# A new list of steps, chunks turned by DMA and a second way out of PSUM in a fused H3 + FFN kernel

## The chip, the cores and the metric

The kernel runs on one core of one Trainium2 chip. The metric is the device time of one execution in microseconds (us). A profiled execution gives the span from the first to the last instruction and, beside it, its own device time, which also holds the little that lies around the span.

## The reference

Sequence length S = 2048, width D = 640, hidden width F = 1728, everything in bf16 at the borders. The input x is normalised once (xn) and used twice: as the gate of a long convolution and as the input of a feed-forward network (FFN).

```python
xn = layernorm(A_q)                                   # [2048, 640]
# A: short convolution of k with 4 taps, times v, then a long convolution over the sequence, times xn
k_shift = sum_t shift(A_k, t) * A_shift_k[:, t]
kv = k_shift * A_v
y  = irfft(rfft(kv padded to 4096) * rfft(A_ssm_k padded to 4096))[:2048].astype(bf16)
s  = xn * (y + kv * A_ssm_D)
# B: FFN
g  = silu(gelu_tanh(xn @ B_w1 + B_b1) @ B_w2 + B_b2)
out = A_q + s * g
```

## The kernel before, in words

The sequence is laid out as 128 partitions by 16 rows (`x_v = ... "(p j) d -> p j d"`), so "row n" is a [128, 640] tile. Four consecutive rows make a chunk, c = 0 to 3, and the FFN works chunk by chunk. One large SBUF tile `mem` of 111 rows of 640 bf16 holds nearly everything. PSUM is the tile `ps` of 8 banks.

The long convolution is done as a discrete Fourier transform split into two stages by matrix products, since 4096 points are 16 x 256:

- **F1 of the filter** (K side). `cl` loads the filter in five pieces, `d` adds A_ssm_D to its first column, `kt{n}` transposes it on TensorE, `kc{n}` copies it out of PSUM, `kf{n}_{h}` multiplies it by the table `ws2` or `ws0` (cosines and sines, built on chip), `ke{n}_{h}` evacuates, `ks{n}` stores to the DRAM scratch scrK. There are 16 n and 2 h.
- **F1 of kv** (U side). `cm{i}_{j}` multiplies k rows by tap j, `ca` adds, `cv` multiplies by v; `uf`, `ue`, `us` are then as on the K side, into scrU.
- **F2, product, inverse 1.** `fl{k}` loads scrK in another order, `ff{g}` and `fe{g}` are the second stage (g from 0 to 31), `mk{k}` copies the result with odd and even partitions swapped (two DMAs from SBUF to SBUF), `ml{k}` loads scrU, `mu{g}` is its second stage, `mp{g}` the complex product on VectorE, `mc{g}` the first inverse stage, `me{g}` its evacuation, `ms{k}` the store to scrC.
- **Inverse 2 and output.** `yl{n}` loads scrC, `y{n}` is four matmuls with the transposed tables G, `yt{n}` (`gate`) multiplies the result by the row of x, `yo` adds the residual row, which `q{c}` loaded again, and `os` stores the row.

The FFN: `st`, `rs`, `nm` are the layernorm of a row. `tt{c}_{k}` transposes chunk c on TensorE (chunk 0: `tx{r}`, row by row), `te` evacuates it. `h{c}_{ft}` is the first FFN product (14 of them for a chunk, five matmuls of 128x512 each; in chunk 0 six are cut into halves `ha`, `hb`), `he` the GELU, `g{c}_{i}` the second product (8 for a chunk, 14 matmuls of 128x320 each), `ge` the SiLU, `gm` the product with the row of x. `it{i}` transposes eight columns' blocks of a table, `ie` evacuates them.

All steps stand in one string, PLAN, in the order in which they are issued. A word such as `ke0_0/17~a` is a step, the row of `mem` where its result goes (/17), the PSUM banks (@0.1), and the engine of an evacuation (~a ScalarE, ~d VectorE). Under `tc.manual_schedule()` each engine runs its own instructions in exactly this order, and waits for data, rows and banks by semaphores. So a step that waits holds up everything behind it on its engine. The loads, the swaps `mk` and the output stores are issued by SyncE (SP) in list order; the scratch stores ks, us and ms by GpSimd (POOL) in list order.

Three lines matter most for what follows. L189 is the evacuation on ScalarE, L190 the one on VectorE (`evac`, whatever the step); L195 holds the matmuls of kf, uf, ff and mu (`mm2`).

Of the kernel before, what the change touches and what calls it, by code (L numbers as in the profile page):

```python
# [41 lines left out]
ge0_3/1 kt3@3 kf5_0@0.1 kc3/16~a g0_5@2 ca0_3 ks2 ke5_0/9~a ke5_1~d cv0 ks5 kf3_0@4.5 ge0_5/0 kf3_1@0.1 cm1_3/7
uf0_0@6.7 ke3_0/70~a g0_4@3 ke3_1~d gm0_5 ks3 cm1_1/17 ue0_0/66~a uf0_1@4.5 cm3_0/21 ge0_4/2 uf1_0@0.1 uf1_1@6.7
ue0_1~a kt6@2 gm0_4 ca1_1 g0_6@3 us0 ue1_0/19~a kc6/72~d ca1_2 ue1_1~a st2_1 kf4_1@4.5 us1 ge0_6/0 kf6_0@0.1 kt7@2
ke4_1~a tt1_2@3 ca1_3 kf6_1@6.7 kc7/6~a ks4 g0_7@4 st2_3 ke6_0/62~a ke6_1~a cv1 te1_2~a ks6 kf7_0@0.1 ge0_7/2 st2_2
kf7_1@6.7 uf2_0@2.3 ke7_0/9~a kt8@5 h1_9@4 ke7_1~a ue2_0/4~d kc8/15~a ks7 st2_0 uf3_1@0.1 he1_9 uf2_1@6.7 kf8_0@2.3
h1_3@5 ue2_1~d rs2 ke8_0/16~d uf3_0@6.7 he1_3 kt9@4 cm2_3/71 h1_4@2 ue3_0/66~a us2 nm2_2 ue3_1~a nm2_0 kt14@3 nm2_3
he1_4 kf8_1@6.7 us3 nm2_1 h1_0@5 kc9/18~a ke8_1~d kc14/70~a kf9_0@0.1 cm2_1/19 ks8 kf9_1@6.7 he1_0 kt10@2 gm0_6
h1_1@4 ca2_1 ke9_0/68~a ke9_1~a gm0_3 kf14_0@0.1 cm3_1/89 h1_12@3 he1_1 ks9 cm4_0/62 kc10/6~a h1_2@5 ke14_0/7~a
ca3_1 he1_12 cm2_2/9 kf10_1@6.7 kf10_0@0.1 he1_2 kt11@4 cm3_2/11 h1_5@2 ke10_0/4~a ca2_2 ke10_1~a h1_6@3 ca3_2  # L50
kc11/23~a ks10 he1_5 ca2_3 kf11_1@0.1 kf11_0@6.7 he1_6 cm3_3/66 h1_10@2 ke11_0/19~a cv2 ke11_1~a kf14_1@4.5 h1_7@3
ca3_3 he1_10 ks11 ke14_1~a cm4_1/15 uf4_0@6.7 uf5_0@0.1 he1_7 ks14 cv3 uf4_1@4.5 kt12@2 ue5_0/17~a h1_8@3 ca4_1
kc12/89~a ue4_0/9~d uf7_0@0.1 ue4_1~a h1_13@2 ue7_0/11~d he1_8 us4 cm4_3/23 kf12_0@6.7 he1_13 uf6_1@4.5 kf12_1@0.1
cv5 ke12_0/71~a kt13@3 h1_11@2 ke12_1~a cm4_2/25 kc13/90~a ks12 gm0_7 uf7_1@6.7 st3_0 uf6_0@0.1 he1_11 g1_0@3
ue6_0/81~a ca4_2 ue6_1~a cm6_3/69 ue7_1~a us6 kf13_0@0.1 uf5_1@4.5 ca4_3 ge1_0/0 us7 uf10_0@6.7 g1_1@2 cm6_0/83 cv4
ue5_1~a st3_3 ke13_0/15~a kt15@3 us5 uf8_0@4.5 ge1_1/1 uf8_1@0.1 st3_2 ue8_0/67~a g1_2@2 ue10_0/4~a gm1_1 kc15/89~a
ue8_1~d cm6_1/101 kf15_1@4.5 us8 ge1_2/2 kf15_0@6.7 uf10_1@0.1 gm1_2 ke15_0/99~a g1_6@3 ca6_1 ke15_1~a st3_1
ue10_1~a ks15 cm6_2/71 uf9_0@6.7 us10 ge1_6/1 uf9_1@4.5 kf13_1@0.1 ue9_0/97~a rs3 gm1_0 tt2_0@2 ca6_2 ue9_1~a g1_5@3
te2_0/6~d ke13_1~a ca6_3 us9 ks13 nm3_1 uf11_1@6.7 ge1_5/2 nm3_0 uf11_0@4.5 g1_4@2 nm3_2 ue11_0/81~a cv6 ue11_1~a
cm7_1/95 us11 uf13_1@0.1 nm3_3 ge1_4/0 uf12_0@4.5 fl5/10 cm7_0/101 uf12_1@6.7 fl0/12 ue12_0/46~a tt2_2@3 fl1/48  # L60
g1_3@2 gm1_4 te2_2~d ue12_1~a fl13/50 ca7_1 fl15/52 us12 fl2/54 cm7_3/56 uf13_0@4.5 ge1_3/0 gm1_5 g1_7@3 cm7_2/89
ue13_0/58~a ue13_1~a gm1_3 ca7_2 us13 ff10@6.7 gm1_6 ge1_7/2 ff0@4.5 ca7_3 ff11@0.1 fe10/4~a tt2_1@2 fe0/99~d fl4/60
fe11~a it0@3 ff2@6.7 te2_1~a cv7 mk5/14 ff1@0.1 ff3@4.5 ie0/62~d fe1~a h2_5@2 fl3/97 fe2/66~d fl8/68 fe3~a mk0/70
gm1_7 uf15_0@0.1 he2_5 uf14_0@6.7 ue15_0/42~d uf14_1@4.5 h2_13@3 mk1/95 ue14_0/81~d uf15_1@0.1 ue14_1~d he2_13
ff4@6.7 h2_6@2 fe4/83~a ue15_1~d us14 ff5@4.5 us15 he2_6 ff9@6.7 fe5~d fl14/44 ff30@0.1 h2_12@3 fe30/85~d mk2/89
ff6@4.5 he2_12 ff8@0.1 h2_11@2 fe8/10~d fl12/46 fe6/12~a fe9~a ff17@4.5 ff31@0.1 he2_11 mk4/48 ff16@6.7 fe31~d
h2_8@3 fe16/87~a fe17~d fl10/16 ff27@0.1 fl6/18 he2_8 ff26@6.7 ml1/20 h2_9@2 fe26/22~d ml0/24 fe27~a ml2/101
ff28@4.5 he2_9 ff29@6.7 fe28/26~d ff7@0.1 ml4/28 fe29~a h2_0@3 fe7~d fl11/30 ff25@4.5 he2_0 ff24@6.7 h2_1@2
fe24/32~d mk3/34 fe25~a h2_7@3 he2_1 ml3/36 ff20@0.1 he2_7 q3/58 ff13@6.7 fe20/81~d ff12@4.5 h2_4@2 fe12/68~a fl7/56
fe13~d mu3@0.1 he2_4 ff21@4.5 mk6/42 mp3/54 mu0@6.7 fe21~a h2_10@3 q1/50 mu5@4.5 mp0/44 he2_10 mu4@0.1 mk10/97  # L70
h2_3@2 mp4/46 fl9/18 mc0@6.7 he2_3 h2_2@3 ml7/16 me0/101~d mc4@0.1 he2_2 ml8/44 mp5/6 mu6@6.7 me4/8~a g2_1@2 mp6/46
mk8/83 mc5@0.1 ge2_1/0 ff14@4.5 me5~d ff15@6.7 g2_2@3 fe14/89~d ms2 fe15~a gm2_1 mc6@0.1 ge2_2/1 ff22@4.5 gm2_2
me6/6~a mu2@6.7 it1@2 mp2/56 ml5/46 fe22/20~a mu1@0.1 q0/77 g2_0@3 ie1~a ml6/24 mp1/8 mk7/66 ff18@4.5 ge2_0/2
mc2@6.7 fe18/95~d mk12/70 mc1@0.1 me2/99~a gm2_0 it3@2 me1~a ff19@4.5 ie3~d q2/72 mc3@6.7 fe19~a ms0 mu8@0.1 me3~d
g2_4@3 mp8/56 ms1 mu7@4.5 ge2_4/0 mu10@6.7 mp7/8 ml15/18 ff23@0.1 g2_3@2 fe23~a mp10/54 mk11/36 mu12@0.1 ge2_3/1
mc7@4.5 mp12/30 mc10@2.3 me7~a tt3_0@6 me10/101~a ms3 mc8@4.5 gm2_3 gm2_4 mc12@0.1 te3_0/54~d me8/34~a mu16@2.3
# [567 lines left out]
```

## Time and profile before

| | before |
|---|---|
| median of 3 runs | 228.1 us (227.66 to 228.65) |
| profiled execution: its own time | 228.88 us |
| profiled execution: span | 227.1 us |
| mean granted TensorE clock | 0.974 |
| TensorE busy | 206.3 us, 91% of the span |
| VectorE busy | 183.6 us, 81% |
| ScalarE busy | 144.0 us, 63% |
| GpSimd busy | 39.1 us, 17% |
| moved by DMA | 57.62 MB, 254 GB/s over the span |

Busy shares are means over the span. A share of the span says little by itself; the stages of the list have different limits, so the table of busy time by stretches and the chain of waits are read beside it. A row of the chain of waits has start, duration and what ran or was waited for; a row of the timeline also has the idle time before it and its releaser.

### The profile page before, as it was taken

What the parts mean: (1) busy time and instruction counts of PE and PEld (TensorE: products, weight loads), DVE (VectorE), ACT (ScalarE), POOL (GpSimd) and SP (SyncE); (2) the same over time, 40 slices, a digit from 0 to 9 for tenths busy, and PEclk for the clock granted to TensorE, in tenths of its full rate; (3) what the DMA queues carried; (4) which work ended last, traced back from release to release, by engine and by line L of the source; (5) the groups of instructions that cost most, each with busy time, mean ns of one, the idle gap of its engine ahead of it and who ended that gap; (6) DMA issues with size and microseconds to landing.
All of it is one profiled execution on the core that took longest, in us unless ns stands there. A gap on an engine that the chain in (4) does not pass through costs nothing.

```text
span 227.1 us, 3979 instructions
## 1 busy us (share of the span) xinstructions
PE 206.3 (91%) x1430; PEld 134.4 (59%) x1442; DVE 183.6 (81%) x305; ACT 144.0 (63%) x223; POOL 39.1 (17%) x72
## 2 busy tenths in 40 slices
PE   7999950799999999999899999899999999989990
...
PEclk9999995599999999999999999999999999999998
DMA  6999999523444142447999999997796313489982
GB/s 216 378 372 274 411 415 415 240 84 139 184 174 173 75 159 115 179 186 271 325 396 331 309 392 386 299 297 283 249 345 219 115 58 118 175 266 352 392 286 95
DMA packets 27114, 57.62 MB, mean 254 GB/s; under 512 B 2966, under 2 KB 16983, under 8 KB 27094
## 3 DMA queue, kind: packets, MB, share of 16 engines
q1 hardware_dynamic: 23072, 41.62, 52.6%
...
q10 hardware_dynamic: 182, 0.01, 0.1%
...
## 4 chain that ended last, share of the span: by engine, by line
PE 33%; issue 31%; DMA 23%; POOL 5%; DVE 5%; SPq 1%; ACT 1%; POOLq 0%; DVEq 0%; ACTq 0%
PE ps L453 14%; PE ps L195 7%; PE ps L438 7%; DMA w_sb<-in_B_w_dram 6%; DMA mem<-in_A_v_dram 5%; DMA scrC<-mem 5%; DMA mem<-in_A_ssm_k_dram 4%; PE ps L572 3%; POOL scrC L547 3%; PE ps L470 3%; DMA mem<-scrC 2%; DVE mem L576 2%; DMA skp<-in_A_shift_k_dram 1%; POOL scrU L505 1%; DVE mem L580 1%
## 5 line engine op out<-in xcount | busy, mean ns | idle before, releaser
L453 PE MATMUL ps<-w_sb,hT 128*128 128x320 bf16 x448 | 67.2, 303 | 0.0
L438 PE MATMUL ps<-mem,w_sb 128*128 128x512 bf16 (+1 forms) x298 | 65.9, 358 | 0.7
L189 ACT CAST mem<-ps 128x640 bf16<-128x640 f32 x92 | 60.6, 697 | 6.7 <-PE ps L541 2.4
L453 PEld LDWEIGHTS <-hT 128*128 128x128 bf16 x448 | 44.0, 99 | 17.9 <-ACT hT L443 0.3
L531 DVE TENSOR_TENSOR mem<-ps,mem 128x1280 bf16<-128x1280 f32 x32 | 45.9, 1485 | 4.6 <-ACT mem L189 1.4
L443 ACT ACTIVATE hT<-ps,b_f 128x512 bf16<-128x512 f32 (+1 forms) x56 | 37.4, 692 | 14.2 <-PE ps L438 14.1
L438 PEld LDWEIGHTS <-w_sb 128*128 128x128 bf16 x310 | 30.0, 98 | 23.3 <-issue 0.2
L458 ACT ACTIVATE sl<-ps 128x320 bf16<-128x320 f32 x32 | 14.0, 438 | 40.4 <-PE ps L453 35.3
L190 DVE CAST mem<-ps 128x640 bf16<-128x640 f32 x36 | 28.9, 821 | 8.2 <-PE ps L195 5.9
L489 DVE TENSOR_TENSOR mem<-mem 128x1280 bf16<-128x1280 bf16 x32 | 25.4, 818 | 11.4 <-DMA mem<-in_A_k_dram 11.4
L189 ACT COPY mem<-ps 128x640 bf16<-128x640 bf16 (+2 forms) x24 | 17.6, 749 | 12.0 <-PE ps L470 10.8
L195 PE MATMUL ps<-mem,mats 128*128 128x320 bf16 x128 | 23.9, 299 | 1.1 <-DMA mem<-scrK 0.9
L547 POOL DMA_DIRECT2D scrC<-mem x16 | 11.4, 715 | 66.6 <-ACT mem L189 38.3
L195 PE MATMUL ps<-mem 128*128 128x320 bf16 x128 | 22.6, 299 | 0.0
L492 DVE TENSOR_TENSOR mem<-mem 128x1280 bf16<-128x1280 bf16 x24 | 19.4, 816 | 0.1
L540 PE MATMUL ps<-mem,mats 128*128 128x320 bf16 x64 | 18.0, 299 | 0.9 <-DVE mem L531 0.9
L541 PE MATMUL ps<-mem,mats 128*128 128x320 bf16 x64 | 18.0, 299 | 0.0
L483 POOL DMA_DIRECT2D scrK<-mem x16 | 9.0, 563 | 50.2 <-DVE mem L190 28.7
L462 DVE TENSOR_TENSOR mem<-mem,sl 128x320 bf16<-128x320 bf16 x32 | 10.0, 319 | 9.2 <-ACT sl L458 9.1
L195 PEld LDWEIGHTS <-mats 128*128 128x128 bf16 x128 | 12.1, 98 | 8.8 <-DMA mem<-scrK 1.6
L470 PE MATMUL ps<-ident,mem 128*128 128x128 bf16 x80 | 7.8, 235 | 9.9 <-DVE mem L190 9.9
L195 PEld LDWEIGHTS <-mem 128*128 128x128 bf16 x128 | 12.3, 98 | 6.6
...
## 6 DMA issues: line engine op xcount, KB each, us to landing
...
mem<-mem SPq DMA_DIRECT2D x32, 160.0 KB, 5.6
...
mem<-in_A_q_dram SPq DMA_DIRECT2D x7, 640.0 KB, 7.8
```

The lines of the kernel that those rows point to most:

```text
L189: return nc.scalar.copy(out=out_ap, in_=in_ap)
L190: return nc.vector.tensor_copy(out=out_ap, in_=in_ap)
L195: nc.tensor.matmul(out=o[:, h, :], lhsT=lhsT, rhs=rhs[:, h * HALF:(h + 1) * HALF], start=start, stop=stop)
L438: nc.tensor.matmul(out=bank(hname(c, ft))[:, a:b], lhsT=w1_sb[:, t, ft * P:(ft + 1) * P], rhs=rhs, start=(t == 0), stop=(t == DT - 1))
L443: nc.scalar.activation(out=hT[0:M, ft, :], in_=bank(hname(c, ft))[0:M, :], func=ACT.Gelu_apprx_tanh, bias=b1_f[0:M, ft:ft + 1], scale=1.0)
L453: nc.tensor.matmul(out=bank(f"g{c}_{i}")[:, 0:HALF], lhsT=hT[0:M, ft, q * P:(q + 1) * P], rhs=w2_sb[0:M, ft, hs], start=(ft == 0), stop=(f ...
L489: nc.vector.tensor_tensor(out=rows(f"cm{i}_{j}", 2), in0=rows("kz", 2, 3 + 2 * i - j), in1=taps(j), op=ALU.mult)
L492: nc.vector.tensor_tensor(out=rows(f"cm{i}_0", 2), in0=rows(f"cm{i}_0", 2), in1=rows(f"cm{i}_{j}", 2), op=ALU.add)
L531: nc.vector.tensor_tensor(out=rows(f"mp{g}", 2).rearrange("p k (h c) -> p k h c", h=2), in0=banks(f"mu{g}")[:, None, :, :].to_broadcast([P ...
L540: nc.tensor.matmul(out=o[:, h, :], lhsT=I1a, rhs=row(f"mp{g}", ia)[:, hs], start=True, stop=False)
L541: nc.tensor.matmul(out=o[:, h, :], lhsT=I1b, rhs=row(f"mp{g}", ib)[:, hs], start=False, stop=True)
L547: nc.gpsimd.dma_start(out=pair_view(scrC)[k], in_=rows(f"me{2 * k}", 2))
```

## The change

The list PLAN is replaced as a whole, the order, the rows, the banks and the engines of evacuations. In the new list:

- no multiply by a tap (`cm`) stands ahead of the filter's first steps; all 32 stand behind `d` and the first two `kc`. In the old list `cm5_1 cm5_2 cm5_0 cm5_3` and the adds `ca5` stand ahead of `te1_0 te1_1 d`, and so ahead of them on VectorE (`cm5_3` reads rows of `kl1`, the k load issued last of the four, as well as of `kl2`);
- the loads at the start are in another order: one piece of the filter between the two halves of chunk 0, chunk 2 and chunk 1 ahead of the second FFN weight, the k rows behind the whole filter;
- rows of chunk 2 are normalised in the first stage (`st2`, `nm2`), beside chunk 1;
- chunks 2 and 3 are transposed by `xd2` and `xd3`, one DMA transpose each ([128, 2560] from SBUF to SBUF, issued by SP), in place of `tt2`, `te2`, `tt3`, `te3`;
- the two tables are transposed by `ig1` and `ig0`, one DMA transpose each ([128, 2048]), in place of `it0` to `it3` and `ie0` to `ie3`;
- each `y{n}` is followed by `yc{n}`, a copy from PSUM to bf16 in SBUF on ScalarE (into the row of `yl{n}`), and `yt{n}` then reads that copy;
- the warming matmuls are 5 and twice 4 where they were 5 and three times 6, and the early load of the GELU table (`ql`) is gone.

```diff
 PLAN = """
-id dm qs xl0_0/0 xl0_1 io1/4 wu@0 wa0 mh pd/12 wa1 kz/19 wa2 qr xl1/38 wb0 wb1 st0_1 io2 em0@1 klh em1@2 ee0/42~a
-st0_2 kl2 ee1~a em2@3 st0_0 wv0 ee2~a cl0/46 st0_3 sq0 pt@4 wv1 rc0 pb sq1 nm0_0 ql cl2 rc1 w tx0@5 em3@6 wv2
...
-he0_1 h0_6@3 he0_5 kl3 he0_3 h0_10@6 nm1_2 he0_6 nm1_1 h0_11@1 he0_12 vl1/81 nm1_0 nm1_3 he0_10 cm5_1/17 tt1_1@4
-he0_11 h0_8@3 kl1 cm5_2/15 he0_2 cm5_0/13 he0_0 h0_13@1 vl3/85 cm5_3/89 he0_8 ie2/91~a h0_7@2 ca5_1 vl0/66 he0_13
-ca5_2 h0_9@0 he0_7 ca5_3 vl2/95 tt1_0@3 he0_9 g0_0@5 te1_0/99~d te1_1~d xl2/103 d kt1@4 ge0_0/0 kt0@7 kc1/70~d
...
+io1/0 dm qs id xl0_0/8 pd/12 cl0/19 xl0_1 mh wu@0 wa0 kz/35 wa1 qr wa2 xl2/54 w xl1/58 cl4 io2 st0_0 em0@1 ws1/62
+em2@2 wb0 st0_1 pt@3 wv4 wb1 pb sq0 rc0 nm0_0 nm0_1 tx0@4 st0_2 tx1@5 cl2 te0_0/69~a wv4 st0_3 te0_1~a ee0/73~a
+ha3@6 ee2~d cl1 ha5@7 sq1 ws0/77 rc1 em3@3 nm0_2 ha2@2 nm0_3 ee3~d tx2@0 ha0@1 s em1@3 cl3 tx3@4 ha4@5 te0_2~a
+te0_3~a ha1@0 klh ee1~a hb4 st2_3 hb5 ss hb0 ws2/81 sm kl0 hb2 st1_3 hb3 h0_7@4 st1_2 xl3/85 he0_3 hb1 st1_1 h0_12@3
...
+rs2 vl0/12 nm1_1 he0_13 nm1_0 kl2 h0_11@4 nm1_3 he0_6 h0_9@5 he0_2 kl3 nm2_3 nm2_2 he0_11 nm2_1 tt1_0@1 he0_9 nm2_0
+g0_1@0 kl1 te1_0/0~d d vl1/4 kt0@1 ge0_1/0 kt1@7 kc0/16~d g0_0@6 kc1/17~d xd2/62 gm0_1 kf0_1@2.3 ge0_0/1 cm0_3/66
...
+kf1_1@4.5 ge0_2/2 kt2@0 vl3/103 cm1_0/107 ke1_1~a kf3_1@2.3 ig1/68 kf3_0@6.7 g0_3@1 ca0_1 kc2/72~a ks1 ke3_0/109~a
...
+fe14/83~a nm3_0 nm3_3 fe15~a fl2/81 nm3_1 ff19@2.3 ml2/76 ff18@4.5 nm3_2 he2_3 ff11@0.1 ml1/99 gm1_7 h2_4@6
+fe18/101~d xd3/12 fe11~a fe19~d ff16@0.1 he2_4 ff17@4.5 h2_5@7 gm1_2 fe16/78~a fe17~a ff22@2.3 ff7@0.1 he2_5
+fe22/66~d mu1@4.5 h2_6@6 fe7~a mp1/6 mu0@2.3 fl6/16 he2_6 ff23@0.1 fl13/18 h2_0@7 mp0/20 fe23~a fl12/22 fl14/24
...
+mc29@6.7 h3_3@0 me29~a mp31/20 ms14 mc27@2.3 he3_3 mc30@6.7 me27~a mc31@0.1 me30/16~d ms13 h3_10@4 me31~a ms15
+he3_10 g3_7@5 g3_1@4 ge3_7/2 yl10/89 yl1/107 yl12/95 yl13/97 g3_4@2 gm3_7 yl5/99 ge3_1/0 yl14/0 gm3_1 yl11/2 yl6/4
+y10@6.7 ge3_4/1 g3_3@3 gm3_4 yc10 yt10 yo10 yl2/6 y12@0.1 os10 ge3_3/2 y13@4.5 gm3_3 yc12 g3_0@2 yc13 yt12 yo12_1
...
+y8@6.7 ge3_6/2 yo3 os4 y0@0.1 gm3_6 yc8 os3 yo9 y15@4.5 yc0 yt8 os9 g3_5@3 yc15 yo8 yt0 os8 yt15 yo0 yo15_1 ge3_5/0
+os0 yo15_0 os15_1 gm3_5 os15_0 yo14_1 os14
 """
...
+    def inv2_out(n):
+        nc.scalar.copy(out=halves(row(f"yl{n}")), in_=banks(f"y{n}"))
+        at["y", n] = row(f"yl{n}")
+
     def gate(n):
-        nc.vector.tensor_tensor(out=halves(x_row(n)), in0=banks(f"y{n}"), in1=halves(x_row(n)), op=ALU.mult)
+        if ("y", n) in at:
+            nc.vector.tensor_tensor(out=x_row(n), in0=at["y", n], in1=x_row(n), op=ALU.mult)
+        else:
+            nc.vector.tensor_tensor(out=halves(x_row(n)), in0=banks(f"y{n}"), in1=halves(x_row(n)), op=ALU.mult)
```

The functions `x_turn` (xd) and `i2_turn` (ig) stood in the kernel before and were not in its list.

More of the change, by code (lines that the diff above doesn't have):

```diff
@@ L42 @@
[L42 to L76, printed above, removed]
@@ new lines @@
+st1_0 he0_1 h0_13@6 he0_5 st2_1 rs1 he0_12 h0_10@0 he0_7 st2_2 he0_0 h0_8@7 he0_10 st2_0 he0_4 h0_6@3 nm1_2 he0_8
+rs2 vl0/12 nm1_1 he0_13 nm1_0 kl2 h0_11@4 nm1_3 he0_6 h0_9@5 he0_2 kl3 nm2_3 nm2_2 he0_11 nm2_1 tt1_0@1 he0_9 nm2_0
+g0_1@0 kl1 te1_0/0~d d vl1/4 kt0@1 ge0_1/0 kt1@7 kc0/16~d g0_0@6 kc1/17~d xd2/62 gm0_1 kf0_1@2.3 ge0_0/1 cm0_3/66
+kf1_0@4.5 kf0_0@0.1 ke1_0/89~a kt3@7 cm0_2/91 g0_2@6 ke0_0/93~a gm0_0 cm0_0/95 ke0_1~a kc3/18~a cm0_1/97 ks0 vl2/99
+kf1_1@4.5 ge0_2/2 kt2@0 vl3/103 cm1_0/107 ke1_1~a kf3_1@2.3 ig1/68 kf3_0@6.7 g0_3@1 ca0_1 kc2/72~a ks1 ke3_0/109~a
@@ new lines @@
+gm0_2 ca0_2 ke3_1~a cm1_2/35 kt5@0 ks3 ge0_3/0 kf2_0@4.5 kc5/16~a kf2_1@6.7 ca0_3 kt4@1 ke2_0/17~a g0_4@2 cm1_1/97
+kc4/91~a cm1_3/92 ke2_1~a cv0 kf4_1@4.5 ks2 ge0_4/1 kt6@3 ca1_1 kf4_0@0.1 kc6/94~a uf0_0@6.7 g0_5@2 gm0_4 ke4_0/66~a
+ue0_0/37~d ke4_1~a ca1_2 ks4 cm2_2/89 uf1_1@0.1 ge0_5/2 uf1_0@6.7 kf6_0@4.5 ca1_3 ue1_0/12~a g0_6@3 ue1_1~a cm2_1/97
+ke6_0/109~a us1 cm3_1/35 uf0_1@6.7 cm2_0/17 ge0_6/1 kf6_1@0.1 kf5_1@4.5 ue0_1~a ig0/91 kt8@2 gm0_6 tt1_1@3 ke6_1~a
+cv1 us0 kf5_0@6.7 kc8/72~a g0_7@0 ks6 te1_1~d ke5_0/95~a gm0_5 ca2_1 ke5_1~a cm3_0/66 ks5 uf2_0@2.3 ge0_7/1
@@ new lines @@
+uf3_0@6.7 ca2_2 uf3_1@4.5 ue2_0/15~a kt7@1 tt1_2@0 cm2_3/97 kc7/14~a uf2_1@2.3 cm4_1/12 te1_2~a kt9@1 ue3_0/89~a
+h1_1@0 kc9/108~d ue3_1~a ca2_3 ue2_1~a kf7_0@6.7 us3 ca3_1 h1_8@1 ke7_0/37~a us2 cv2 he1_1 kf7_1@4.5 h1_9@2 cm4_3/39
+cm3_2/97 uf4_0@6.7 kt10@3 he1_8 cm4_0/109 h1_4@0 kc10/107~a ue4_0/35~d he1_9 h1_5@1 ca4_1 he1_4 ca3_2 uf4_1@6.7
+ke7_1~a uf5_0@2.3 h1_6@0 he1_5 cm3_3/4 ks7 ue5_0/95~a cm5_0/89 kf9_0@4.5 he1_6 h1_7@1 ke9_0/12~d ue4_1~a ca3_3
+kf8_1@2.3 he1_7 us4 kf8_0@4.5 uf5_1@6.7 cm6_1/97 h1_10@0 ue5_1~a cv3 ke8_0/41~a us5 kf9_1@6.7 ke8_1~d h1_2@1 he1_10
@@ new lines @@
+gm0_7 ke9_1~a ks8 cm4_2/14 uf6_0@4.5 he1_2 uf6_1@2.3 ks9 kf10_0@6.7 gm0_3 h1_0@0 ue6_0/16~a ca4_2 ue6_1~d kf10_1@4.5
+he1_0 kt11@1 ca4_3 us6 uf7_0@2.3 kc11/43~a h1_13@0 ke10_0/4~d ke10_1~a cv4 kt12@1 ue7_0/6~a ks10 kf11_0@6.7
+uf7_1@4.5 he1_13 kc12/72~d uf8_0@2.3 ke11_0/37~d h1_11@1 ue7_1~a cm5_2/35 ue8_0/107~a us7 uf9_0@6.7 he1_11
+kf11_1@4.5 cm6_0/95 h1_3@0 ue9_0/39~a cm5_1/41 ke11_1~a kt13@1 ca6_1 kf12_0@2.3 he1_3 ks11 kt14@6 kc13/18~d
+uf8_1@4.5 ke12_0/14~a h1_12@7 ca5_1 ue8_1~a cm5_3/12 kc14/66~a kf13_1@0.1 us8 kf13_0@2.3 ca5_2 kf12_1@4.5 he1_12
@@ new lines @@
+ff29@4.5 fe27~d ff28@0.1 h2_9@7 fe28/99~a fe29~d ml14/40 ff31@2.3 he2_9 ff30@0.1 ff13@4.5 fe30/6~d h2_10@6 fe31~a
+q1/42 fe13~d mu4@0.1 he2_10 ml4/97 ff21@2.3 ff20@4.5 g2_5@7 fe20/4~a mp4/95 ml6/46 fe21~a mk6/89 mu6@4.5 ge2_5/0
+mu7@2.3 mp6/48 mk5/109 mc4@0.1 g2_1@6 ml5/16 me4/18~a mp7/20 q2/22 mc6@4.5 ge2_1/1 gm2_5 q3/62 mc7@0.1 gm2_1
+me6/26~d mu5@2.3 me7~a g2_3@7 mp5/30 ms3 ml7/34 mk14/95 mu8@4.5 ge2_3/2 mu9@0.1 mp8/36 mc5@2.3 ml10/52 g2_6@6 me5~a
+mp9/50 ms2 mk11/48 mc8@2.3 ge2_6/0 gm2_3 mu12@4.5 gm2_6 mc9@0.1 mk10/20 me8/76~d g2_4@7 me9~a mp12/72 mk9/97 ms4
@@ new lines @@
+mu10@2.3 ge2_4/1 mu11@0.1 mp10/30 mc12@4.5 g2_2@6 me12/28~a ml8/26 mp11/103 mc10@4.5 ge2_2/2 gm2_4 mc11@2.3 gm2_2
+me10/36~a mk13/50 mu13@0.1 me11~d g2_0@7 mp13/74 ml9/18 ms5 q0/103 mu15@4.5 ge2_0/0 mu14@2.3 mp15/16 mc13@0.1
+mk12/30 g2_7@6 me13~a gm2_0 ms6 ml11/72 mp14/76 mc15@0.1 ge2_7/1 mu20@4.5 gm2_7 mk15/46 mc14@6.7 mp20/109 h3_8@2
+me14/89~a me15~a mu21@6.7 mc20@4.5 he3_8 ms7 mp21/107 ml13/74 mu28@0.1 h3_1@3 mp28/34 mu16@6.7 me20/36~a h3_13@2
+he3_1 mp16/32 mc21@4.5 he3_13 mu17@0.1 me21~a h3_9@3 ml12/16 mp17/82 ms10 mc16@6.7 he3_9 mu18@4.5 me16/76~a h3_11@2
```

50 lines of the change are left out of this document (26 added, 24 removed).

## The prediction, made before the changed kernel ran

> **What bounds the kernel now.** I read the page first, for where TensorE is not busy, then busy time by stretches cut at those places, then the chain of waits and the list of waits inside them. Two parts of the page: 40 slices of 5.7 us each, and the DMA queues.
>
> ```profile
> PE   7999950799999999999899999899999999989990
> PEclk9999995599999999999999999999999999999998
> DMA  6999999523444142447999999997796313489982
> ...
> q1 hardware_dynamic: 23072, 41.62, 52.6%
> ```
>
> TensorE is full apart from one hole in slices 6 and 7 and the end, and its granted clock halves in the hole. The same, cut at the hole (31.00, 41.20), at the first reload of scrK (104.7) and at the last store to scrC (195.1); columns are TensorE, weight loads, VectorE, ScalarE, GpSimd, clock, DMA share, GB/s:
>
> ```profile
> 0.00:31.00 31.00, 28.94 (x200) 17.95 (x203) 21.77 (x65) 26.07 (x33) 6.85 (x20) 1.00 0.98 337
> 31.00:41.20 10.20, 0.30 (x3) 0.14 (x1) 4.46 (x7) 0.44 (x1) 0.00 (x0) 0.67 1.02 415
> 41.20:104.70 63.50, 63.34 (x459) 43.20 (x462) 60.97 (x110) 52.19 (x89) 18.67 (x32) 0.97 0.39 153
> 104.70:195.10 90.40, 88.11 (x593) 55.91 (x598) 75.33 (x81) 59.18 (x90) 12.88 (x19) 1.00 0.79 271
> 195.10:227.10 32.00, 25.65 (x181) 17.23 (x179) 21.02 (x44) 6.16 (x11) 0.72 (x1) 0.98 0.78 273
> ```
>
> From 41.2 to 195.1 TensorE is the bound (63.34 of 63.50, 88.11 of 90.40), with VectorE close behind it (60.97 of 63.50). Then what the hole waits for, in the list of waits and the chain:
>
> ```profile
> DVE mem L489 <- DMA mem<-in_A_k_dram: 11.4, 2, 10.4
> PE ps L470 <- DVE mem L190: 9.9, 1, 9.9
> ...
> 20.59 8.46 DMA mem<-in_A_ssm_k_dram
> 29.07 10.80 DMA mem<-in_A_v_dram
> 39.87 1.29 DVE mem L190 x2
> 41.20 1.22 PE ps L470 x10
> 42.42 3.07 PE ps L453 x14
> ...
> 66.26 0.81 PE ps L195 x6
> 67.07 1.08 PE ps L438 x5
> ...
> 157.68 0.45 PE ps L419 x8
> 158.87 1.90 PE ps L453 x14
> ```
>
> TensorE stands at the first `kt` (L470) from 31.0 on. The filter has landed at 29.05, yet `d` and te1 (L190) stand behind `cm5_3` on VectorE, a tap multiply (L489) that waits 10.4 us for a k chunk. So the hole is a matter of order: the filter's steps queue behind a load they don't need. (The chain puts the landing down to v, the list of waits to k.) The last rows give the pace of one instruction on the path: 0.136 us for a 128x320 matmul, 0.216 for 128x512, 0.056 for a transpose. At half clock, just behind the hole, 14 FFN matmuls took 3.07 instead of 1.90, and ten transposes 1.22 instead of 0.62.
>
> **Front and hole.** VectorE around the hole, with its norms and statistics:
>
> ```profile
> 23.96 2.30 DVE L489 TENSOR_TENSOR mem<-mem 128x1280 bf16<-128x1280 bf16 x3 [0.96 <-DMA mem<-in_A_k_dram]
> 36.67 0.83 DVE L489 TENSOR_TENSOR mem<-mem 128x1280 bf16<-128x1280 bf16 x1 [10.41 <-DMA mem<-in_A_k_dram]
> ...
> L489 DVE TENSOR_TENSOR mem<-mem 128x1280 bf16<-128x1280 bf16 x32 | 25.4, 818 | 11.4 <-DMA mem<-in_A_k_dram 11.4
> L392 DVE BATCH_NORM_STATS2 stats<-mem 128x6 f32<-128x320 bf16 x32 | 13.8, 473 | 0.0
> L408 DVE TENSOR_SCALAR mem<-mem,mv,rstd 128x640 bf16<-128x640 bf16 x16 | 6.2, 440 | 1.5 <-POOL rstd L398 1.5
> ```
>
> In the new list only norms, te1_0 and `d` precede `kt` on VectorE. Is the data there? In list order the loads up to the filter's last piece were 9.50 MB before (sizes from the shapes) and landed at 29.05, so 0.327 MB/us; now they are 9.01 MB, so 27.5 us. Is VectorE there? It was busy 21.77 of the first 31 us; four more rows of statistics and norms (4 x (2 x 0.473 + 0.440) = 5.5), less the three tap multiplies that ran by then (2.3), make 25 of 31. ScalarE was busy 26.07 of 31 and loses an early table load and a table evacuation while it takes one more tap or chunk copy. So TensorE should reach `kt` at about the 31.0 of before and go on by 32. The hole's 10.2 us shrink to 1.0: **-9.2**. With no idle stretch like that the clock stays up, and the half-clock extras go (1.17 + 0.60): **-1.8**. The k halo and first k chunk, 1.14 MB further, land at 31.0, before VectorE's first multiply of them, so the old wait isn't just moved. The first FFN product also starts earlier, as it needs only two rows turned, but ScalarE paces this stage; I take 0, bounds -2 and +2. Ten fewer warming matmuls fill waits only.
>
> **Turns by DMA.** Taken from TensorE are 40 transposes (tt2, tt3) and 32 (it): 72 x 0.056 = 4.0 us. Their ten evacuations go too. But the stage from 41.2 to 104.7 has VectorE at 60.97. From the first `kt` to the first `fl` the new list has eight rows of statistics and norms less (8 x 1.386 = 11.1 us) and, of the work that ran in the hole or ahead of it, seven tap multiplies and six adds more (13 x 0.82 = 10.6); two evacuations go over to ScalarE. So VectorE stays at 59 to 61, and a stage of about 61 us holds back some of what TensorE could give. I count half: **-2.0**, bounds 0 and -4.0.
>
> No transfer of the trace transposes, so `xd` (640 KB) and `ig` (512 KB) are bounded by copies:
>
> ```profile
> mem<-mem SPq DMA_DIRECT2D x32, 160.0 KB, 5.6
> mem<-in_A_q_dram SPq DMA_DIRECT2D x7, 640.0 KB, 7.8
> out_dram<-mem SPq DMA_DIRECT2D x15, 160.0 KB, 3.7
> ```
>
> By the same bytes an `xd` lands after 7.8 us; by four SBUF-to-SBUF swaps one after the other, after 22. I take 8, nearest to the row of equal size. `xd2`, `ig1` and `ig0` come between 32 and the first reload, where DMA is busy 0.39 of the time, and their results are needed by h2 and by the end: they cost nothing until they fill that stretch, over 15 us each. On SP only vl2 and vl3, wanted late, stand behind them. `xd3` is different: it waits for nm3 on VectorE, and then six reloads `fl`, queued behind it on SP, wait too, in the stretch where the DMA row reads 9. Their cover in the list is at least 5.1 us of TensorE work between a reload and its F2 product (4.6 before). Its bytes take 2 us at 337 GB/s; I take half as hidden: **+1**, bounds 0 and +17 (22 less about 5 of cover).
>
> On this the Trainium skill gives two answers. "VectorE: DVE Perf Modes", section "The three transpose paths", has 390 ns on TensorE and 1309 ns by DMA for one 128x128 block, and advises TensorE where PSUM will do: against this change. As an estimate, 20 blocks one after another are 26 us, and `xd3` alone would cost some 21. "Advanced Engine Details and Errata", section "X-Bar Transpose (TRN2)", says such transfers run as fast as others. The trace bears out neither, as it holds none.
>
> **The end.**
>
> ```profile
> L576 DVE TENSOR_TENSOR mem<-ps,mem 128x640 bf16<-128x640 f32 x16 | 12.6, 820 | 1.1 <-PE ps L572 1.0
> L189 ACT CAST mem<-ps 128x640 bf16<-128x640 f32 x92 | 60.6, 697 | 6.7 <-PE ps L541 2.4 <-PE ps L195 1.5 <-DMA scrC<-mem 0.8
> L580 DVE TENSOR_TENSOR mem<-mem 128x640 bf16<-128x640 bf16 x12 | 5.6, 486 | 0.0
> L580 DVE TENSOR_TENSOR mem<-mem 128x320 bf16<-128x320 bf16 x8 | 2.5, 323 | 0.1
> L462 DVE TENSOR_TENSOR mem<-mem,sl 128x320 bf16<-128x320 bf16 x32 | 10.0, 319 | 9.2 <-ACT sl L458 9.1
> L458 ACT ACTIVATE sl<-ps 128x320 bf16<-128x320 f32 x32 | 14.0, 438 | 40.4 <-PE ps L453 35.3 <-DVE mem L580 3.3 <-issue 1.6
> ...
> 195.13 0.72 POOL L547 DMA_DIRECT2D scrC<-mem  x1 [0.22 <-issue]
> 198.64 5.75 SPq L565 DMA_DIRECT2D mem<-scrC  x11
> 201.91 1.25 PE L572 MATMUL ps<-mem 128*128 128x320 bf16 x8
> 220.53 1.25 PE L572 MATMUL ps<-mem 128*128 128x320 bf16 x8
> ```
>
> A gate cost VectorE 820 ns; now ScalarE takes 697 (it has 26 us free of 32) and VectorE 486, the row of an all-SBUF bf16 operation of that size: VectorE loses 16 x 0.334 = 5.3 us in a stage where it was busy 21.0 and wrote the last rows (two gates back to back behind the last matmul at 221.8). After that matmul 5.3 us remained; now it is an FFN product, followed by a SiLU (438), `gm` (319), `yo` (323) and a store (160 KB, 3.7): 4.8, so -0.5. TensorE has 1.1 less after the last scrC store. Against it, 5.7 us of TensorE work stand between that store and the first `y`, where store and reload took 201.9 - 195.1 = 6.8: +0.9. Sum **-0.7**, bounds -3 and +2; the 16 reloads and stores (7.9 MB) take 24 us at 337 GB/s and forbid more.
>
> **Sum.** -9.2 - 1.8 + 0 - 2.0 + 1 - 0.7 = -12.7. The profiled execution took 228.88 (span 227.1), so 216.2; its own time is 0.8 above the median of 228.1, which gives 215.4.
>
> **Rivals.**
>
> *Turns hold up the queue* (slower). If an `xd` needs around 22 us, as four swaps in a row, and SP or the DMA engines are held, +17 replaces +1 at `xd3`: 231.4. If the first three fill their stretch too, several us more. It takes over from about 18 us for one `xd`, where 13 us are eaten. For: a block per transfer, small packets, a place in saturated DMA. Against: q1 moved 1.8 KB a packet in 83 ns (52.6% of 16 x 227.1 us over 23072), so 640 KB even in 256 B packets, at that time each, is 13 us. Chance 0.20. The Trainium skill's 1309 ns (page and section above) would make it 215.4 - 1 + 21 = 235, an estimate; it is the same case.
>
> *Half of it comes back as new waits.* VectorE and TensorE will both be nearly full from 32 to 93 us, and the order is new throughout: 3 us more there and 3 at the reloads and the first `y`, which have thin covers, give 221.4. For: VectorE at 60.97 of 63.50 leaves no slack. Against: before ran just as tight and lost 0.2. Chance 0.17.
>
> *All of it.* Transposes count in full (-2 more), the front's -2 and the end's -2.3: 209. Chance 0.06.
>
> The forecast keeps 0.57. That the list doesn't do what it says (another k load still ahead of `kt`) is nearly excluded by its order; 0.02 of that, at 228, is within the rest.
>
> **How the numbers follow.** No change means within 0.5%, 1.1 us, about what can be measured here. Forecast, half and all lie below 227: 0.57 + 0.17 + 0.06, less 0.04 of spill from the half: 0.76. Slower: 0.20 + 0.01. Same: 0.03. The range runs from 208 (all of it) to 232 (the turns rival's first price), and leaves out the worse half of that rival, 0.1, and a little below. The forecast's own range is 211 to 219.
>
> **What would show it.** Right: no idle stretch at L470 over 2 us, clock 1.0 throughout, the first scrK reload at about 94 us, the last scrC store (195.1 before) at about 184, `xd` landing in under 10 us. Wrong: TensorE (L195) or VectorE waiting on reloads of scrK right behind `xd3`; SP's issue of a transpose lasting many us; swaps landing far above their 5.6 us; or a hole at the first tap multiply.

## The result and the profile after

The changed kernel takes 219.41 us (median of 4 runs, 218.91 to 222.13) where the kernel before, in the same set, takes 228.38. The ratio is 0.9617, 95% interval 0.9517 to 0.9718. The forecast was 215.4, with 208 to 232 as its range. Absolute times drift by some tenths of a per cent from set to set, so the experiments below are compared by their ratio to the kernel before, run beside each of them. The ratios leave disturbed executions out (the profiled one of run 4, 227.95 us, is among these), while the medians are of all.

The profiled execution took 219.46 us, span 217.7. The same parts of the page as before:

```profile
PE   3889999939989999999999999999999999998991
PEclk9999999976999999999999999999999999999998
DMA  6999999999999563548999899999997212489993
...
q1 hardware_dynamic: 32416, 43.98, 65.9%
```

The hole of slices 6 and 7 is gone. A smaller one stands in slice 9, and the clock is lower in slices 9 and 10. The DMA row now reads 9 up to slice 13, where before it fell to 5, 2, 3 from slice 8 on. The stretches, cut at the first `kt` (30.7), the first reload of scrK (99.1) and the last store to scrC (187.5); columns as in the prediction:

```profile
0.00:30.70 30.70, 25.56 (x176) 15.88 (x177) 27.33 (x79) 24.31 (x31) 11.27 (x22) 1.00 0.97 327
30.70:99.10 68.40, 63.64 (x448) 41.85 (x447) 58.33 (x90) 54.55 (x91) 15.68 (x29) 0.95 0.87 239
99.10:187.50 88.40, 88.25 (x565) 54.60 (x563) 76.14 (x89) 53.27 (x83) 14.05 (x21) 1.00 0.85 283
187.50:217.70 30.20, 24.57 (x177) 16.70 (x175) 17.06 (x44) 15.63 (x26) 0.72 (x1) 0.98 0.81 283
```

Against the prediction's table: up to `kt` 30.7 (41.2 with the hole), then 68.4 (63.5), 88.4 (90.4), 30.2 (32.0). So 10.5 us were gained up to `kt` and 3.8 in the last two stages, and the stage behind `kt` lost 4.9. The list of waits and the chain say where:

```profile
DVE mem L489 <- DMA scrK<-mem: 9.4, 2, 5.2
PE ps L195 <- DVE mem L495: 3.7, 1, 3.7
...
36.26 9.33 DMA scrK<-mem
45.65 0.71 issue
46.35 0.83 DVE mem L495
47.23 0.71 PE ps L195 x2
47.94 3.73 PE ps L453 x14
```

A store to scrK, issued at 36.26, lands after 9.3 us. A tap multiply (L489) wants to write into rows that a scrK store still reads, and VectorE waits 5.2 us for them (and 4.2 us once more, up to 56.75). `cv0` (L495) stands behind it, and TensorE's `uf0_0` (L195) waits for that, 3.75 us. Behind the hole the clock is halved once more: 14 FFN matmuls take 3.73 us instead of 1.90. What SP did in that time, from the timeline, and how long the scrK stores of GpSimd took to land, before (first line) and after (second):

```profile
32.37 14.96 SPq L430 DMA_TRANSPOSE mem<-mem  x1
47.39 1.09 SPq L386 DMA_DIRECT2D mem<-in_A_v_dram  x2
48.58 21.17 SPq L559 DMA_TRANSPOSE mem<-mem  x2
115.10 6.67 SPq L430 DMA_TRANSPOSE mem<-mem  x1
...
DMA to landing us min/median/max: 2.4/2.4/2.9
DMA to landing us min/median/max: 2.5/3.0/15.0
```

The late stores coincide with `xd2` and `ig1`, whose issue holds SP for 15.0 and 14.7 us (`ig0` took 6.3 of the 21.17). That is a coincidence in time so far; the experiments ask whether it is the cause. The two landing rows alone can't tell, because the stores of before began only at 48.4, when the k and v loads were over, and those of the change at 36.3, among these loads.

### The profile page after: what moved, and what is told of

Same layout as the page of the kernel before. It is cut to its first block, busy times and chain, and to the rows that moved or that the text cites. A ratio compares the mean times of both kernels' runs of the same rounds, so it can differ in the third digit from the quotient of the medians.

```text
span 217.7 us, 3850 instructions
## 1 busy us (share of the span) xinstructions
PE 202.0 (93%) x1360; PEld 129.0 (59%) x1360; DVE 178.9 (82%) x301; ACT 147.8 (68%) x231; POOL 41.7 (19%) x72
## 4 chain that ended last, share of the span: by engine, by line
PE 65%; DMA 14%; DVE 6%; issue 5%; ACT 4%; POOL 2%; SPq 2%; POOLq 0%; DVEq 0%
PE ps L438 21%; PE ps L453 19%; PE ps L195 12%; DMA scrK<-mem 4%; PE ps L572 3%; DMA mem<-scrC 3%; PE ps L541 3%; PE ps L540 3%; DMA scrU<-mem 3%; DMA mem<-scrU 3%; DVE mem L190 3%; ACT mem L189 2%; PE ps L470 1%; DMA scrC<-mem 1%; PE ps L255 1%
## 5 line engine op out<-in xcount | busy, mean ns | idle before, releaser
L438 PE MATMUL ps<-mem,w_sb 128*128 128x512 bf16 (+1 forms) x310 | 68.1, 358 | 1.2 <-ACT mem L189 0.8
L443 ACT ACTIVATE hT<-ps,b_f 128x512 bf16<-128x512 f32 (+1 forms) x56 | 37.2, 691 | 13.2 <-PE ps L438 13.0
L489 DVE TENSOR_TENSOR mem<-mem 128x1280 bf16<-128x1280 bf16 x32 | 25.6, 827 | 9.4 <-DMA scrK<-mem 9.4
L195 PE MATMUL ps<-mem 128*128 128x320 bf16 x128 | 24.2, 307 | 4.0 <-DVE mem L495 3.7
L195 PE MATMUL ps<-mem,mats 128*128 128x320 bf16 x128 | 23.8, 299 | 0.1
L492 DVE TENSOR_TENSOR mem<-mem 128x1280 bf16<-128x1280 bf16 x24 | 19.7, 829 | 0.0
L195 PEld LDWEIGHTS <-mem 128*128 128x128 bf16 x128 | 12.4, 100 | 11.5 <-DVE mem L495 4.3
L195 PEld LDWEIGHTS <-mats 128*128 128x128 bf16 x128 | 12.1, 98 | 8.9 <-DMA mem<-scrK 1.3
L189 ACT COPY mem<-ps 128x640 bf16<-128x640 bf16 (+1 forms) x18 | 12.1, 700 | 5.2 <-DMA scrK<-mem 2.6
L505 POOL DMA_DIRECT2D scrU<-mem x16 | 8.6, 539 | 29.4 <-ACT mem L189 20.5
```

The lines of the kernel that those rows point to most:

```text
L189: return nc.scalar.copy(out=out_ap, in_=in_ap)
L195: nc.tensor.matmul(out=o[:, h, :], lhsT=lhsT, rhs=rhs[:, h * HALF:(h + 1) * HALF], start=start, stop=stop)
L438: nc.tensor.matmul(out=bank(hname(c, ft))[:, a:b], lhsT=w1_sb[:, t, ft * P:(ft + 1) * P], rhs=rhs, start=(t == 0), stop=(t == DT - 1))
L443: nc.scalar.activation(out=hT[0:M, ft, :], in_=bank(hname(c, ft))[0:M, :], func=ACT.Gelu_apprx_tanh, bias=b1_f[0:M, ft:ft + 1], scale=1.0)
L489: nc.vector.tensor_tensor(out=rows(f"cm{i}_{j}", 2), in0=rows("kz", 2, 3 + 2 * i - j), in1=taps(j), op=ALU.mult)
L492: nc.vector.tensor_tensor(out=rows(f"cm{i}_0", 2), in0=rows(f"cm{i}_0", 2), in1=rows(f"cm{i}_{j}", 2), op=ALU.add)
```

## The experiments

Two theories were put against each other. **Theory A**: the early DMA transposes delay the scratch stores, and rows that wait for the stores stop VectorE and then TensorE. **Theory B**: the k and v loads saturate the DMA engines there anyhow, and the stage is long because its engines are tight. Beside them, the order alone (one step moved in the old list), the copies, and the fourth transpose were measured apart.

| kernel | ratio to before | 95% interval | median us |
|---|---|---|---|
| the change | 0.9617 | 0.9517 to 0.9718 | 219.41 |
| no early turns | 0.9267 | 0.9227 to 0.9307 | 212.84 |
| before, one step moved | 0.9545 | 0.9492 to 0.9597 | 219.51 |
| change, gate from PSUM | 0.9727 | 0.9677 to 0.9776 | 223.03 |
| turns later in the list | 0.9638 | 0.9570 to 0.9705 | 224.84 |
| turns held back, apart | 0.9299 | 0.9245 to 0.9354 | 213.29 |
| no turns at all | 0.9262 | 0.9205 to 0.9320 | 212.25 |
| copies for turns | 0.9275 | 0.9213 to 0.9338 | 212.44 |
| before, one step moved, and copies of y | 0.9544 | 0.9477 to 0.9610 | 219.17 |
| turns held back, together | 0.9307 | 0.9224 to 0.9390 | 212.71 |

**1. Without the early turns.**

```diff
     def x_turn(c):
+        if c == 2:
+            return
...
     def i2_turn(i):
-        nc.sync.dma_start_transpose(out=table(G[i]), in_=flat(("ws2", "ws0")[i], 4)[:, 0:NJ * P])
+        return
```

> The changed kernel without its three early DMA transposes (chunk 2 and both tables); chunk 2's first FFN product then reads the rows unturned, and the last inverse stage reads the second FFN weight in place of the tables, so the output is another one; every other instruction is kept. Theory A (the turns hold up the scratch stores, and rows that wait for those stores hold up VectorE and TensorE): no hole at 43 us, no half clock after it, scrK stores landing in 2.4 to 3 us throughout, the stage from the first kt to the first reload 61 to 62 us instead of 68.4, time 212 to 214 us. Theory B (the k and v loads saturate the DMA engines there anyway, and the stage is long because VectorE and ScalarE are tight): the stores stay late and the time stays at 217 to 219 us.

Ratio 0.9267, theory A's case. Its stretch from `kt` (30.7) to the first reload (93.0), and the landing of its scrK stores:

```profile
30.70:93.00 62.30, 60.56 (x450) 41.25 (x452) 58.84 (x92) 54.21 (x92) 15.90 (x29) 1.00 0.60 236
...
DMA to landing us min/median/max: 2.4/3.0/7.0
```

62.3 us instead of 68.4, the clock at 1.00, the DMA engines busy 0.60 of it instead of 0.87. The prediction's 61 us for this stage was right for a list whose turns cost nothing. Theory B has fallen: the loads are still there. One detail of the expectation was too neat. A few stores still landed after up to 7.0 us here, beside the loads alone, and VectorE waited 2.7 us for one of them; TensorE kept its clock. The turns took the longest landing from 7.0 to 15.0 us.

**2. One step moved in the old list.**

```diff
-h0_13@1 vl3/85 cm5_3/89 he0_8 ... he0_7 ca5_3 vl2/95 tt1_0@3
+h0_13@1 vl3/85 he0_8 ... he0_7 vl2/95 tt1_0@3
...
-ke0_1~a gm0_0 ks1
+ke0_1~a gm0_0 cm5_3/89 ca5_3 ks1
```

> The kernel before with two words of its list moved: cm5_3 and ca5_3, which wait for the late k chunk, go from ahead of d to behind gm0_0. Nothing else of the change is in it. If the hole at 31 us is only a matter of order on VectorE, it closes but for 1 us and the clock stays up: 228.4 - 9.2 - 1.8 = 217.4 us, range 216 to 219, which would be at least as fast as the whole change. If the hole has another cause behind it (the k loads, the filter), another wait takes its place and the time stays above 223.

Ratio 0.9545 (range expected: 216 to 219; measured 219.51 beside a kernel before of 229.44, or 218.0 by the ratio). Two words moved in the old list give as much as the whole change; the interval even lies a little lower, though it overlaps the change's. A second execution for a profile:

> The kernel before with the two moved words once more, for a profile: kt should follow the first FFN product at 31 us without a hole, the clock should stay at 1.0, and the stage from kt to the first reload should be about 62 to 64 us; time about 218 us.

It took 217.84 us. From its list of waits and its timeline of TensorE:

```profile
DVE mem L489 <- DMA mem<-in_A_k_dram: 2.3, 2, 1.7
...
29.59 2.07 PE L453 MATMUL ps<-w_sb,hT 128*128 128x320 bf16 x14
31.49 0.88 PE L470 MATMUL ps<-ident,mem 128*128 128x128 bf16 x10
32.21 2.07 PE L453 MATMUL ps<-w_sb,hT 128*128 128x320 bf16 x14
```

The same multiply waits 1.7 us at most instead of 10.4, `kt` follows the FFN product at once, and the next FFN product runs at full clock. So the hole came from the order on VectorE.

**3. The gate from PSUM again.** All `yc` words are taken out of the new list.

```diff
-y10@6.7 ge3_4/1 g3_3@3 gm3_4 yc10 yt10 yo10 yl2/6 ...
+y10@6.7 ge3_4/1 g3_3@3 gm3_4 yt10 yo10 yl2/6 ...
```

> The changed kernel without the ScalarE copies of the inverse result: the gate reads PSUM again, as before. If the copies are what shortened the last stage (30.2 us after the last scrC store, 32.0 before), VectorE takes 16 x 0.33 = 5.3 us more there and the time rises by 2 to 5 us. If reloads of scrC set the pace of the last stage, it stays within 1 us.

Ratio 0.9727 against 0.9617, with intervals that overlap, so the place of the difference in the trace has to carry the verdict. The stretch from the last scrC store to the end, and the gate's group:

```profile
187.40:221.10 33.70, 24.81 (x177) 16.82 (x174) 21.65 (x44) 5.47 (x10) 0.72 (x1) 0.94 0.72 254
...
L583 DVE TENSOR_TENSOR mem<-ps,mem 128x640 bf16<-128x640 f32 x16 | 12.7, 816 | 0.3 <-PE ps L572 0.3
```

33.7 us instead of 30.2, with all of the difference there (its other stages are within 0.2 us of the change's). Six other runs of the new list with the copies have 29.5 to 31.6 us in this stage, so 33.7 stands outside their spread, but the price of the copies is known no better than that. In the changed kernel the two groups that take the place of this one are:

```profile
L576 ACT CAST mem<-ps 128x640 bf16<-128x640 f32 x16 | 10.2, 703 | 1.7 <-PE ps L572 1.4
L581 DVE TENSOR_TENSOR mem<-mem 128x640 bf16<-128x640 bf16 x16 | 7.5, 488 | 2.1 <-ACT mem L576 2.1
```

488 and 703 ns were forecast as 486 and 697. The copies are worth about 2.5 (by the ratios) to 3.5 us (by these two profiles) in this list.

**4. Turns later in the list.** `xd2`, `ig1` and `ig0` are moved behind `us4`, `ks8` and `ks13`.

```diff
-kc1/17~d xd2/62 gm0_1 ... kf3_1@2.3 ig1/68 kf3_0@6.7 ... ue0_1~a ig0/91 kt8@2
+kc1/17~d gm0_1 ... kf3_1@2.3 kf3_0@6.7 ... ue0_1~a kt8@2
...
+he1_7 us4 xd2/62 kf8_0@4.5 ... ke9_1~a ks8 ig1/68 cm4_2/14 ... ke12_1~a ks13 ig0/91 kf14_0@2.3
```

> The changed kernel with the three early DMA transposes issued later, at about 72, 76 and 88 us in place of 32, 49 and 63, behind the last loads of v; everything is computed. Theory A with the loads as accomplice (stores are late only where turns, loads and stores meet): no hole at 43 us and 3 to 6 us faster. Theory A without (a turn delays stores wherever it stands): the hole moves to 75 to 95 us and the time stays within 2 us. Theory B: no change.

Ratio 0.9638, no gain, and the expectation was built on an error of mine. A later place in the list is not a later time on SP:

```profile
32.11 1.78 SPq L386 DMA_DIRECT2D mem<-in_A_v_dram  x3
35.19 14.25 SPq L430 DMA_TRANSPOSE mem<-mem  x1
49.54 19.85 SPq L559 DMA_TRANSPOSE mem<-mem  x2
```

SP runs through its own instructions as soon as their waits allow. Between the v loads and the first scrK reload it has nothing but the turns, so they are issued at 35.2 and 49.5, 2.8 and 1.0 us behind where they were, and `xd2` still meets the v loads. The experiment says nothing on turns at 72 us. It does exclude one other cause: in the change `xd2` holds SP and so two v loads back to 47.4, here all v loads are issued ahead of it, by 33.9, and nothing is won. (In the change's list of waits nothing waits for a v load either.)

**5. Turns held back, apart.** To give SP something to wait for, VectorE writes one column of each target first, at the wanted place of its order.

```diff
     def x_turn(c):
+        if c == 2:
+            nc.vector.memset(flat(xt(c), 4)[:, 0:1], 0.0)
...
     def i2_turn(i):
+        nc.vector.memset(flat(G[i], 4)[:, 0:1], 0.0)
...
+ke7_0/37~a us2 xd2/62 cv2 ... ke8_0/41~a us5 ig1/68 kf9_1@6.7 ... he1_3 ks11 ig0/91 kt14@6
```

> The changed kernel with its three early DMA transposes really held back: each one's target gets a one-column write by VectorE just before it in the list, so that SP waits for VectorE's place in time (about 58, 68 and 78 us). Everything is computed. The k and v loads have landed by then and the turns no longer meet them or each other. Theory A with the loads as accomplice: scratch stores land within 6 us, no hole near 43 us, the first reload at 94 to 95 us, ratio to the kernel before 0.93 to 0.945 (0.962 for the change, 0.927 without early turns). Theory A without: a turn delays the stores about it wherever it stands, VectorE waits for rows again, ratio 0.95 to 0.965.

Ratio 0.9299, with an interval clear of the change's: 213.29 us with everything computed, within 0.4% of the run without early turns.

```profile
58.48 4.86 SPq L432 DMA_TRANSPOSE mem<-mem  x1
68.09 13.08 SPq L562 DMA_TRANSPOSE mem<-mem  x2
...
30.70:92.70 62.00, 60.19 (x447) 41.01 (x449) 58.38 (x93) 54.25 (x92) 15.80 (x29) 1.00 0.76 260
...
DMA to landing us min/median/max: 2.4/3.7/7.0
```

The stage takes 62.0 us. The longest landing of a scrK store is 7.0 us (last line), where it was 15.0.

**6. Turns held back, together.** All three stand behind `us2`, at 58.6 to 71.9 us, one right after the other.

```diff
-us2 xd2/62 cv2 ... us5 ig1/68 kf9_1@6.7 ... ks11 ig0/91 kt14@6
+us2 xd2/62 ig1/68 ig0/91 cv2 ... us5 kf9_1@6.7 ... ks11 kt14@6
```

> As the run with the turns held back, but all three at the first one's place, about 58 us, one right behind the other, when the k and v loads have landed. If a turn is harmful only while large loads are in flight, the ratio stays at 0.928 to 0.935. If it is turn behind turn (their packets filling the queue for 10 us and more), scratch stores land late again around 60 to 75 us, VectorE waits for rows, and the ratio is 0.94 to 0.96.

Ratio 0.9307. Turn behind turn does no harm here; the scrK stores then land after 7.3 us at most. So three turns in a row are harmless when they start behind the big loads, and harmful when the first starts among them. One thing stays open. In run 4 a store issued at 51.9 us still landed after 13.2, although the loads had landed by 49.3; a turn that has met the loads seems to pass its delay on to the next, and no run separates that from the loads themselves.

**7. Copies for turns.** The four turns become plain copies of the same bytes, at the change's own places.

```diff
-        nc.sync.dma_start_transpose(out=flat(xt(c), 4).rearrange("p (q s) -> p q s", s=P), in_=flat(f"xl{c}", 4))
+        nc.sync.dma_start(out=rows(xt(c), 4), in_=rows(f"xl{c}", 4))
...
-        nc.sync.dma_start_transpose(out=table(G[i]), in_=flat(("ws2", "ws0")[i], 4)[:, 0:NJ * P])
+        nc.sync.dma_start(out=table(G[i]), in_=table(("ws2", "ws0")[i]))
```

> The changed kernel with each of its four DMA transposes replaced by a plain copy of the same bytes between the same rows of SBUF, at the same place of the list; what is copied is not turned, so the output is another one. If the turns are dear because of their 256 B packets (9216 of them at 41 ns on average), the copies, with packets twenty times as long, take about 2 us each, the stores land in 2.5 to 4 us, and the ratio is 0.927 to 0.935. If it is the bytes or the place in the queue, the ratio stays near 0.96.

Ratio 0.9275. The same bytes, rows and place in the queue cost nothing measurable when they are copied. The transpose itself is the expense. Packets of before, of the change and of this kernel:

```profile
DMA packets 27114, 57.62 MB, mean 254 GB/s; under 512 B 2966, under 2 KB 16983, under 8 KB 27094
...
DMA packets 36457, 59.96 MB, mean 275 GB/s; under 512 B 12310, under 2 KB 26327, under 8 KB 36438
...
DMA packets 27690, 59.96 MB, mean 282 GB/s; under 512 B 3031, under 2 KB 17048, under 8 KB 27671
```

The turns bring 9344 packets of under 512 B, the copies 65. What they take of the 16 engines shows in queue q1, here of the change, of run 5, of this kernel and of run 8 (next), which has no turn at all:

```profile
q1 hardware_dynamic: 32416, 43.98, 65.9%
q1 hardware_dynamic: 32416, 43.98, 61.6%
q1 hardware_dynamic: 23648, 43.98, 58.7%
q1 hardware_dynamic: 23072, 41.62, 55.8%
```

Share times 16 engines times span gives 2295, 2089, 1994 and 1889 us (for run 5, 0.616 x 16 x 212.0). Over run 8 the four turns so took 406 us of engine time in the change, 25 us of all 16, but 200 us, or 12.5 of all 16, when the first three started behind the loads; the copies took 105, or 6.6. The same packets thus cost 43 ns each in the change and 21 in run 5. The price isn't one of the packet alone.

**8. No turns at all.** As run 1, and `xd3` is left out too.

```diff
     def x_turn(c):
-        if c == 2:
-            return
+        return
```

> As the run without early turns, and without the fourth DMA transpose (chunk 3) as well, whose first FFN product then reads its rows unturned; the output is another one. It prices the fourth turn, which stands among the reloads. The prediction's +1 with bounds 0 and +17: ratio 0.922 to 0.927 if it costs 0 to 1 us; below 0.915 if it costs over 3 us.

Ratio 0.9262 against 0.9267 with `xd3`: the fourth turn, the one that the prediction feared, costs nothing that can be measured. With intervals of half a per cent to each side, a microsecond would not have shown.

**9. One step moved, and the copies.** Run 2 with each inverse result copied by ScalarE first.

```diff
     def gate(n):
-        nc.vector.tensor_tensor(out=halves(x_row(n)), in0=banks(f"y{n}"), in1=halves(x_row(n)), op=ALU.mult)
+        nc.scalar.copy(out=halves(row(f"yl{n}")), in_=banks(f"y{n}"))
+        nc.vector.tensor_tensor(out=x_row(n), in0=row(f"yl{n}"), in1=x_row(n), op=ALU.mult)
```

> The kernel before with the two moved words (cm5_3, ca5_3) and the ScalarE copy of each inverse result ahead of its gate, and nothing else; everything is computed. The moved words gave a ratio of 0.9545; the copies gave the changed kernel about 1.1%. If both add, 0.943 to 0.948, faster than the whole change. If the reloads of scrC set the pace of the end in this order, 0.952 to 0.958.

Ratio 0.9544, the same as without the copies (0.9545). In the old order they bring nothing measurable, in the new one 2.5 to 3.5 us. Why the old order doesn't profit wasn't settled; no run separates its order of reloads from its order of FFN products.

The version that beats both kernels is run 5 (and run 6, level with it). Against run 2, the one step moved, it is 2.6% faster by the ratios. Stage by stage, the profile of run 5 against that of run 2's second execution has 30.7 for 31.4 up to `kt`, 62.0 for 64.2 up to the first reload, 87.7 for 88.5 and 31.6 for 32.0. So most of the gain lies behind `kt`. At the end the copies mainly make good what the new order loses without them (33.7 in run 3). The parts of the new list, among them the transposes taken off TensorE, weren't measured apart.

## Why the prediction was right, and where it wasn't

**Front and hole: right, slightly better.** `kt` was to follow by 32 us with 1.0 us of the hole left. It follows the FFN product at 30.7 without a gap. Run 2 shows the reason to be the named one: two words moved close the hole.

**Half clock: right as a mechanism, wrong in the outcome.** The clock stays up where the hole was, but the new hole at 43.5 halves it again, and 1.8 us that were to go came back (3.73 instead of 1.90 for one FFN product).

**Early turns: the step that failed.** The text took 8 us for a turn and said that the early ones "cost nothing until they fill that stretch, over 15 us each". They cost 6.1 us in that stage (68.4 against 62.3 in run 1) and 1.2 in the next (88.4 against 87.2), together 3.6% of the time by the ratios 0.9617 and 0.9267. Two things went wrong. The first is the size. The profile's rows tell the landing of one early turn of the change, 8.3 us for `ig0`, issued last, at 63.5. For `xd2` and `ig1` the semaphore times in its trace give 24.5 and 19.8 us from issue to landing, and run 4 has 24.7 for its `xd2`. So two of the three were over the 15 us that the text itself named. The second is the stretch, which was taken as one with spare DMA time, 0.39 busy on average. Its beginning has none: in run 1, without the turns, the engines were busy 0.99 of 36 to 48 us with the k and v loads. Stores that land late hold rows which VectorE wants soon after (`cm1_3` writes a row that `ks0` still reads). The "turns" rival named that price ("if the first three fill their stretch too, several us more"), but put the main harm at `xd3`. Among the text's signs of being wrong, "SP's issue of a transpose lasting many us" is what the profile showed.

**`xd3`: +1 forecast, nothing measured** (run 8 against run 1), and +1 can't be told from nothing there. SP was held 6.7 us, and TensorE was busy 88.25 of the stage's 88.4. This stage took 90.4 before, but run 2's profile, with the old list's transposes on TensorE, has 88.5 as well. So these 2.0 us are not shown to come from the turns.

**The end: right in kind, short in size.** -0.7 forecast, -1.8 measured (30.2 against 32.0), and without the copies it would have been +1.7 (33.7). The operations' durations were right to a few ns. TensorE's work (24.57 for 25.65, -1.1) and the time behind its last matmul (4.8 for 5.3, -0.5) came as forecast. The term that failed is the +0.9 for a first `y` held up by store and reload. Its 6.8 us weren't the time of store and reload: in the kernel before, TensorE was busy with FFN matmuls up to that `y`. In the change the first `y` starts 5.7 us behind the last scrC store (187.53 to 193.23), right behind the FFN product.

**The sum.** By the stages the forecast had 32, 61 to 62, about 90 and 31. Measured are 30.7, 68.4, 88.4 and 30.2. All but the second came out better than said, and the miss of 4 us in the total is the second stage's 7 us less the others' gains of 3.7, and the 0.8 us that the forecast took off for its profile. That the total came out so near owes something to luck, since gains elsewhere hid half of the failed step. At 219.4 the kernel stands just outside the forecast's own range of 211 to 219 and near the "half of it comes back" rival (221.4), whose new waits did come, from a cause that the text had priced at nothing. Without the early turns' price the kernel would have stood at about 212, inside that range.

**How long a turn takes.** From issue to landing, in the profile's rows of the change, of run 5, and of the early `xd2` of run 4:

```profile
mem<-mem SPq DMA_TRANSPOSE x4, 8.3
...
mem<-mem SPq DMA_TRANSPOSE x4, 6.1
...
DMA to landing us min/median/max: 24.7/24.7/24.7
```

The first row rests on one landing (`ig0`), the second on two (6.5 and 5.8). With `xd3` of run 1 (9.0) that is 0.3 to 0.5 us for each 128x128 block clear of the large loads, and 1.2 us a block among them; the `ig0` of run 6, issued right behind `ig1`, took 11.9. The two pages of the Trainium skill were cited as contradicting each other. "VectorE: DVE Perf Modes", section "The three transpose paths", gives 1309 ns for a block, as an estimate 21 to 26 us for a turn of 16 or 20. The turns that met the loads come near it and the others don't, so it is no price of the turn alone. "Advanced Engine Details and Errata", section "X-Bar Transpose (TRN2)", has transposes as fast as other transfers. Run 7 and run 5 don't bear that out: the turns took twice a copy's engine time clear of the loads (12.5 against 6.6 us) and four times among them (25). No run has the new list with these transposes on TensorE, so whether a turn at 58 us beats TensorE isn't shown. At 32 us the three turns cost more than the 4.0 us of TensorE time that the text counted for all four.
